# Expert keys of an attention-and-experts kernel by products of 512 columns, pooled values on 64x64 tiles, and another order of the first stage

## The chip, the cores and the metric

The kernel runs on one core of one Trainium2 chip. The metric is the time of one execution on the device in microseconds (us), lower is better. A core has five engines that work side by side, each in its own order: TensorE (PE in the profile, its weight loads PEld), VectorE (DVE), ScalarE (ACT), GpSimd (POOL) and SyncE (SP), which here issues all transfers between main memory and the on-chip memory (SBUF). TensorE writes its products to PSUM, which is divided into banks of 512 fp32 columns.

## What is computed

Eight batches of 576 positions go through an attention with 8 heads of 64 channels, and then through a gated mixture layer (512 channels, 1024 hidden). The reference, cut to what matters:

```python
q_d = q.reshape(B, H, Sd, factor, D).mean(axis=3)      # factor 4, Sd = 144; the same for k_d, v_d
out_d = sm_attn(q_d, k_d, v_d)                         # softmax attention on the pooled 144
out_up = np.repeat(out_d, factor, axis=2)
mask = np.abs(pos[:, None] - pos[None, :]) < factor    # local attention, |i - j| < 4
out_local = np.matmul(attn, v)
x = out_up + out_local                                 # heads side by side: (B, S, 512)
xk = mu_k * x + (1.0 - mu_k) * x_prev                  # x_prev: x shifted by one position
xr = mu_r * x + (1.0 - mu_r) * x_prev
k = np.maximum(xk @ w_k, 0.0)
v = k * k @ w_v
r = 1.0 / (1.0 + np.exp(-(xr @ w_r)))
return r * v
```

## The kernel before

**The work.** The 32 pairs of heads (4 for each batch) pass one after the other through an attention part, and the 18 chunks of 256 positions through an expert part. A pair n has its loads (`load_raw` for q and k, `load_v4` for the values to be pooled, `load_windows` for the local values), pooling on GpSimd, scores on TensorE (`score_pe`, `down_pe`, `down_last`), two softmaxes on the three other engines, `down_turn` (transposes on TensorE) and `av_pe`, the products with the values. From pair 5 on, `run_pe` puts the scores of pair n and the value products of pair n-1 into one run. `av_out` adds the upsampled pooled part and the local part to the tile xt of the batch.

**The expert part.** It works in fp32r, with each fp32 operand split into a high and a low part, and three products instead of one. For chunk c `mix_*` makes xk and xr (high and low), `k_pe(c, f)` makes the keys of one of 8 groups f of hidden channels: 12 products of 256 columns into one PSUM tile, (weight high, xk high), (weight high, xk low), (weight low, xk high) for each of 4 slices of the channels. `k_relu`, `k_high` (a square and a copy, ScalarE) and `k_low` (a difference, VectorE or GpSimd) make the squared keys in two parts, kh and kl. `v_pe(c, f)` adds 6 products of 512 columns to the two accumulators of the chunk, `r_pe` makes the gate with 24 products, `gate`, `store_mul` and `store_out` end the chunk. "k of f", "v of f" below stand for `k_pe(c, f)` and `v_pe(c, f)`.

**The weights.** 20 pieces (8 of w_k, 8 of w_v, 4 of w_r, 512 KB each) come as 64-bit numbers. For each, ScalarE (`weight_scale`) and VectorE (`weight_shift`, `weight_tail`, `weight_sign`, lines 287 to 296) make fp32 of it, and then the two parts.

**What sets the order.** All of these are tasks with an engine, a cost, a rank and the tiles they read and write. The class `Plan` lays them out in time by its own costs: at each step the task that can start first, and among those of one engine that can start by then the one with the lowest rank. Ranks are due times written out in the code (`PER`, `XLEAD`, `FETCH` and so on). The order found is then fixed on every engine by dependencies, so on the chip an engine takes its instructions in just that order, and one that waits holds up all behind it. The plan also gives each PSUM tile one of six banks; the scores have two more. `fill` puts products without use (`keep_warm`, tile ps_x) into TensorE's planned gaps of the first 100 us.

**The stages.** At first the loads, the weights and the four pairs of batch 0 run (nothing of the expert part can start before the xt of batch 0 is whole). Then the chunks run with the pairs of the following batches between them, and the last three or four chunks run alone.

## Time and profile before

| | us |
|---|---|
| median of 3 runs | 705.48 (703.69 to 705.82) |
| the profiled execution | 705.88 |
| its span, from the first to the last instruction | 703.9 |
| TensorE busy | 674.1 (96% of the span) |
| VectorE, ScalarE, GpSimd busy | 465.5, 439.3, 303.3 |
| transfers | 62.21 MB, mean 88 GB/s |

The table is that of one profiled execution beside the three timed ones. Busy times of TensorE hold its products without use too, and a busy TensorE is one in which some product is in the pipeline. 2.0 us of the profiled time lie outside the span.

### The profile page before, as it was taken

To read this page: it belongs to the slowest core of one execution; us is meant where nothing else is said; L and a number is where in the kernel's file an instruction comes from. 1 tells how busy PE (TensorE), PEld (TensorE's weight loads), DVE (VectorE), ACT (ScalarE), POOL (GpSimd) and SP (SyncE) were. 2 spreads that over 40 slices of the span, in tenths; PEclk is the share of its full clock that TensorE was granted. 3 is DMA by queue.
4 is the path that set the end of the run, shared out by engine and by line. 5 is a ranking of instruction groups with operands and counts; after the bars stand their busy time and mean duration, and the time that the engine had idled before them with its cause. 6 is when DMAs were issued, how large, how long until landed. Compare 5 with 4: busy or idle time off the path is not lost.

```text
span 703.9 us, 18635 instructions
## 1 busy us (share of the span) xinstructions
PE 674.1 (96%) x7467; PEld 576.9 (82%) x7467; DVE 465.5 (66%) x855; ACT 439.3 (62%) x1095; POOL 303.3 (43%) x374
## 2 busy tenths in 40 slices
PE   7888977999999999999999999999999999999997
PEld 5565866888888888888888888888888888988986
...
GB/s 149 181 197 273 221 148 132 124 79 116 68 114 75 107 56 128 54 93 44 87 87 52 59 115 88 88 77 104 71 101 40 53 2 31 1 30 31 1 32 31
DMA packets 221849, 62.21 MB, mean 88 GB/s; under 512 B 205122, under 2 KB 214594, under 8 KB 221762
## 3 DMA queue, kind: packets, MB, share of 16 engines
...
q14 instruction: 28, 0.23, 0.1%
...
## 4 chain that ended last, share of the span: by engine, by line
PE 69%; DVE 11%; ACT 5%; SPq 4%; POOL 4%; DMA 3%; issue 3%; DVEq 0%; POOLq 0%; ACTq 0%
PE ps_g L674 24%; PE acc L719 22%; PE ps_r L704 12%; PE ps_v L581 3%; SPq L335 3%; PE ps_a L449 2%; PE ps_v L575 2%; DMA v<-in_v_dram 1%; ACT ad L533 1%; ACT L533 1%; DVE ps_w L291 1%; PE ps_a L516 1%; DMA wv<-in_moe_w_v_dram 1%; DVE kl L693 1%; PE ps_a L509 1%
## 5 line engine op out<-in xcount | busy, mean ns | idle before, releaser
L674 PE MATMUL ps_g<-xkh,wk 128*128 128x256 f32 x1152 | 229.5, 285 | 2.9 <-ACT kk L679 2.0
L674 PEld LDWEIGHTS ps_g<-xkh,wk 128*128 128x128 f32 x1152 | 186.6, 190 | 11.4 <-ACT kk L679 4.9
L719 PE MATMUL acc<-wv,kh 128*128 128x512 f32 x576 | 181.2, 396 | 0.0
L674 PE MATMUL ps_g<-xkl,wk 128*128 128x256 f32 x576 | 162.6, 282 | 0.7 <-DVE xkl L666 0.7
L693 DVE TENSOR_TENSOR kl<-kk,kh 128x256 fp32r<-128x256 f32 x119 | 64.0, 538 | 118.0 <-ACT kh L686 110.8
L719 PEld LDWEIGHTS acc<-wv,kh 128*128 128x128 f32 x576 | 101.0, 189 | 18.9 <-issue 2.5
L674 PEld LDWEIGHTS ps_g<-xkl,wk 128*128 128x128 f32 x576 | 109.9, 191 | 3.9 <-DVE xkl L666 0.9
L719 PE MATMUL acc<-wv,kl 128*128 128x512 f32 x288 | 112.6, 391 | 0.1
L679 ACT ACTIVATE kk<-ps_g 128x256 f32<-128x256 f32 x144 | 54.5, 379 | 84.2 <-PE ps_g L674 77.9
L704 PE MATMUL ps_r<-wr,xrh 128*128 128x512 f32 x288 | 90.2, 394 | 1.7 <-POOL wr L323 1.4
L693 POOL TENSOR_TENSOR kl<-kk,kh 128x256 fp32r<-128x256 f32 x25 | 18.5, 742 | 124.2 <-PE acc L719 96.1
L719 PEld LDWEIGHTS acc<-wv,kl 128*128 128x128 f32 x288 | 54.1, 188 | 12.8 <-DVE kl L693 0.8
L686 ACT ACTIVATE kh<-kk 128x256 fp32r<-128x256 f32 x144 | 60.2, 418 | 4.6
L685 ACT ACTIVATE kk<-kk 128x256 f32<-128x256 f32 x144 | 60.1, 418 | 4.5
L704 PEld LDWEIGHTS ps_r<-wr,xrh 128*128 128x128 f32 x288 | 52.5, 188 | 12.4 <-POOL wr L323 1.8
L477 POOL TENSOR_TENSOR sm<-sm,mx 128x384 f32<-128x384 f32 x28 | 24.4, 873 | 83.1 <-DVE sd L539 60.6
L704 PE MATMUL ps_r<-wr,xrl 128*128 128x512 f32 x144 | 56.1, 390 | 0.0
L523 DVE TENSOR_REDUCE mxd<-ps_a 128x3 f32<-128x432 f32 x32 | 19.3, 604 | 48.8 <-PE ps_a L449 39.6
L422 POOL TENSOR_TENSOR v<-v 72x512 f32<-72x512 f32 x32 | 44.6, 1395 | 16.0 <-DMA v<-in_v_dram 15.8
L423 POOL TENSOR_TENSOR vd<-v 72x256 f32<-72x256 f32 x32 | 27.7, 866 | 51.0 <-PE ps_v L575 49.6
L413 POOL TENSOR_TENSOR tk<-kz 64x288 f32<-64x288 f32 (+1 forms) x56 | 41.9, 748 | 16.1 <-DVE kz L386 12.5
L533 ACT ACTIVATE ad<-ps_a,mxd 128x144 f32<-128x144 f32 x96 | 35.3, 376 | 20.3 <-DVE mxd L524 17.5
...
## 6 DMA issues: line engine op xcount, KB each, us to landing
...
qraw<-in_q_dram SPq DMA_DIRECT2D x128, 72.0 KB
kraw<-in_k_dram SPq DMA_DIRECT2D x128, 72.0 KB
...
```

The lines of the kernel that those rows point to most:

```text
L413: nc.gpsimd.tensor_tensor(out=tk[h], in0=k4[:, :, 0:2], in1=k4[:, :, 2:4], op=ALU.add)
L422: eng.tensor_tensor(out=v4[:, :, 0:128], in0=v4[:, :, 0:128], in1=v4[:, :, 128:256], op=ALU.add)
L423: eng.tensor_tensor(out=vd, in0=v4[:, :, 0:64], in1=v4[:, :, 64:128], op=ALU.add)
L477: nc.gpsimd.tensor_tensor(out=s3, in0=s3, in1=mx[:, :, None].broadcast_to([P, 12, 32]), op=ALU.subtract)
L533: nc.scalar.activation(ad[:, t, :], ps[:, t, :], AF.Exp, scale=1.0 / 128, bias=mx[:, t:t + 1], accum_out=sd[:, t:t + 1])
L674: nc.tensor.matmul(ps, w_k_part(p, f, w), y[:, p, :], start=(m == 0), stop=(m == len(mm) - 1))
L679: nc.scalar.activation(kk, kq[c, f], AF.Relu)
L685: nc.scalar.activation(kk, kk, AF.Square)
L686: nc.scalar.activation(kh, kk, AF.Copy)
L693: eng.tensor_tensor(out=kl, in0=kk, in1=kh.bitcast(F32), op=ALU.subtract)
L704: nc.tensor.matmul(ps, y[:, p, P * t:P * t + P], ws[f"r{p}"][:, w, :], start=(m == 0), stop=(m == len(mm) - 1))
L719: nc.tensor.matmul(accs[c][t], x[:, P * t:P * t + P], ws[f"v{f}"][:, w, :], start=(f == 0 and m == 0), stop=(f == NF - 1 and m == 2))
```

## The change

**Keys.** From chunk 2 on (`WIDE = 2`) the high and low parts of xk stand in one tile, and `k_pe` makes for each slice one product of 512 columns, weight high with both halves, into a PSUM tile of 2 x 256 columns, and then four of 256 columns, weight low with xk high, onto the first half. That is 8 products and 8 weight loads for each k in place of 12 and 12, of the same columns in sum. Since the two halves have to be added, ScalarE copies the second half to SBUF (`k_part`), VectorE adds the first one to it (`k_sum`, line 744), and `k_relu` then works on SBUF. The rest of the chain is as it was.

**Pooled values.** The 144 pooled positions were two blocks of 72. They now stand in a tile of 112 rows and one whose rows 96 to 127 hold the other 32, with rows 64 to 95 kept at zero, so that the products of `av_pe` have contractions of 64, 48 and 64 rows, and all lie on 64x64 tiles of TensorE, as the local products behind them do: 6 products in place of 4. The upper and the lower halves go to different PSUM tiles, and a new VectorE step (`av_two`, 144 columns) adds them. `load_v4` has two transfers in place of one, and `clear_v` sets the two value tiles to zero at the start.

**Order.** The table SHIFT changes ranks of tasks of the first chunks, pairs and weights; a few costs in the plan change too, and with the other tasks the whole order is laid out anew.

```diff
+WIDE = 2
 DXPOOL = 2
+KA = 112
+SHIFT = {
+    "av_up.5": -7.5, "c.0": 19.8, "c.1": 84, "c.3": 112.3, "down_sum.5": 35.8, "down_top.2": 2.2,
+    "down_top.4": 8.3, "fetch_weight.10": 4.7, "fetch_weight.12": 26.2, "fetch_weight.17": -87.2,
...
+    def shift(self, name, args):
+        if not args:
+            return SHIFT.get(name, 0.0)
+        i, more = args[0], args[1:]
+        full = f"{name}.{more[0]}" if name in ("mix_part", "mix_add", "mix_high", "mix_low") else name
+        kind = "c" if name in OF_CHUNKS else "w" if "weight" in name else "p"
+        if kind != "w" and i > (3 if kind == "c" else 9):
+            return 0.0
+        keys = [f"{kind}.{i}", f"{full}.{i}"]
+        if name in ("k_pe", "v_pe", "k_relu", "k_high", "k_low", "r_pe"):
+            keys.append(f"{name}.{i}.{more[0]}")
+        if name == "load_raw":
+            keys.append(f"{name}{more[0]}.{i}")
+        return sum(SHIFT.get(x, 0.0) for x in keys)
+
     def add(self, eng, us, rank, f, *args, r=(), w=(), new=(), dma=0.0, lock=None):
-        t = dict(eng=eng, us=us, rank=rank, f=f, args=args, new=list(new), dma=dma, deps=set(),
+        t = dict(eng=eng, us=us, rank=rank + self.shift(f.__name__, args), f=f, args=args, new=list(new), dma=dma, deps=set(),
                  id=len(self.tasks), name=f.__name__, lock=lock)
...
+    def clear_v():
+        for x in v4s:
+            nc.gpsimd.memset(x, 0.0)
...
         b, p = divmod(n, NP)
-        v4 = wp.tile([72, 4, 256], F32, tag="v4", name="v4", bufs=2)
+        v4 = v4s[n % 2]
         base = (b * H + 2 * p) * S * D
-        nc.sync.dma_start(v4, bass.AP(v.tensor, base, [[4 * D, 72], [288 * D, 4], [1, 4 * D]]))
+        nc.sync.dma_start(v4[0:KA, 0:2, :], bass.AP(v.tensor, base, [[4 * D, KA], [S * D, 2], [1, 4 * D]]))
+        nc.sync.dma_start(v4[96:P, 2:4, :], bass.AP(v.tensor, base + KA * 4 * D, [[4 * D, 32], [S * D, 2], [1, 4 * D]]))
         st.setdefault(n, {})["v4"] = v4
 
...
         d = st[n]
         if n < NP:
-            d["ps_t"] = [pp.tile([72, 288], F32, tag=plan.bank[f"pst{n}{kt}"], name="ps_t", bufs=1) for kt in range(2)]
+            d["ps_t"] = [pp.tile([P, 288], F32, tag=plan.bank[f"pst{n}{kt}"], name="ps_t", bufs=1) for kt in range(2)]
         else:
             ps = pp.tile([P, 1024], F32, tag="att", name="ps_t", bufs=1)
-            d["ps_t"] = [ps[0:72, 512 * kt:512 * kt + 288] for kt in range(2)]
-        for kt, ps in enumerate(d["ps_t"]):
-            ak = [d["ad"][:, t, 72 * kt:72 * kt + 72] for t in range(3)]
+            d["ps_t"] = [ps[:, 512 * kt:512 * kt + 288] for kt in range(2)]
+        for kt, (ps, ks) in enumerate(zip(d["ps_t"], (slice(0, KA), slice(16, 144)))):
+            d["ps_t"][kt] = ps = ps[0:ks.stop - ks.start]
+            ak = [d["ad"][:, t, ks] for t in range(3)]
...
-            nc.scalar.activation(d["adT"][:, kt, :], d["ps_t"][kt], AF.Copy)
+        d["adT"] = aT = wp.tile([P, 2, 288], F32, tag="adT", name="adT", bufs=1)
+        nc.scalar.activation(aT[0:KA, 0, :], d["ps_t"][0], AF.Copy)
+        nc.scalar.activation(aT[64:P, 1, :], d["ps_t"][1][64:P], AF.Copy)
...
 
         d = st[n]
         pv = [pp.tile([P, 432], F32, tag=plan.bank[f"pv{n}{x}"], name="ps_v", bufs=1) for x in ("", "b")]
-        for kt in range(2):
+        aT, up = d["adT"], slice(288, 432)
+        for r, h in enumerate((slice(0, 64), slice(64, KA))):
             for e in range(2):
-                nc.tensor.matmul(pv[0][64 * e:64 * e + 64, 288:432], d["vd"][:, 2 * e + kt, :],
-                                 d["adT"][:, kt, 144 * e:144 * e + 144], start=(kt == 0), stop=(kt == 1))
+                nc.tensor.matmul(pv[r][64 * e:64 * e + 64, up], d["vd"][h, e, :],
+                                 aT[h, 0, 144 * e:144 * e + 144], start=True, stop=(r == 0))
+        h = slice(64, P)
+        for e in range(2):
+            nc.tensor.matmul(pv[1][64 * e:64 * e + 64, up], d["vd"][h, 2 + e, :], aT[h, 1, 144 * e:144 * e + 144],
+                             start=False, stop=True)
         for g in range(NG):
             for r in range(2):
                 h = slice(64 * r, 64 * r + 64)
...
+    def av_two(n):
+        d = st[n]
+        nc.vector.tensor_tensor(out=d["up"], in0=d["pv"][1][:, 288:432], in1=d["up"], op=ALU.add)
 
...
-        h = wp.tile([P, NP, CT], F32R, tag=nm + "h", name=nm + "h", bufs=2 if nm == "xk" else 1)
-        nc.scalar.activation(h, mixes[c][nm], AF.Copy)
-        xs[c, nm] = [h]
+        x = wp.tile([P, 2, NP, CT], F32R, tag=nm, name=nm, bufs=2 if nm == "xk" else 1)
+        nc.scalar.activation(x[:, 0], mixes[c][nm], AF.Copy)
+        xs[c, nm] = x
...
-        xs[c, nm].append(lo)
+        x = xs[c, nm]
+        nc.vector.tensor_tensor(out=x[:, 1], in0=mixes[c][nm], in1=x[:, 0].bitcast(F32), op=ALU.subtract)
 
     def k_pe(c, f):
-        xh, xl = xs[c, "xk"]
-        ps = pp.tile([P, CT], F32, tag=plan.bank[f"g{c}.{f}"], name="ps_g", bufs=1)
-        mm = [(w, y, p) for p in range(NP) for w, y in ((0, xh), (0, xl), (1, xh))]
-        for m, (w, y, p) in enumerate(mm):
-            nc.tensor.matmul(ps, w_k_part(p, f, w), y[:, p, :], start=(m == 0), stop=(m == len(mm) - 1))
+        x = xs[c, "xk"]
+        if c < WIDE:
+            ps = pp.tile([P, CT], F32, tag=plan.bank[f"g{c}.{f}"], name="ps_g", bufs=1)
+            mm = [(w, y, p) for p in range(NP) for w, y in ((0, 0), (0, 1), (1, 0))]
+            for m, (w, y, p) in enumerate(mm):
+                nc.tensor.matmul(ps, w_k_part(p, f, w), x[:, y, p, :], start=(m == 0), stop=(m == len(mm) - 1))
+        else:
+            ps = pp.tile([P, 2, CT], F32, tag=plan.bank[f"g{c}.{f}"], name="ps_g", bufs=1)
+            for p in range(NP):
+                nc.tensor.matmul(ps, w_k_part(p, f, 0), x[:, :, p, :], start=(p == 0), stop=False)
+            for p in range(NP):
+                nc.tensor.matmul(ps[:, 0], w_k_part(p, f, 1), x[:, 0, p, :], start=False, stop=(p == NP - 1))
         kq[c, f] = ps
 
+    def k_part(c, f):
+        ps = kq[c, f]
+        kk = wp.tile([P, CT], F32, tag="kk", name="kk")
+        nc.scalar.activation(kk, ps[:, 1], AF.Copy)
+        kq[c, f] = ps, kk
+
+    def k_sum(c, f):
+        ps, kk = kq[c, f]
+        nc.vector.tensor_tensor(out=kk, in0=ps[:, 0], in1=kk, op=ALU.add)
+        kq[c, f] = kk
+
     def k_relu(c, f):
-        kk = wp.tile([P, CT], F32, tag="kk", name="kk")
-        nc.scalar.activation(kk, kq[c, f], AF.Relu)
-        kq[c, f] = kk
+        if c < WIDE:
+            kk = wp.tile([P, CT], F32, tag="kk", name="kk")
+            nc.scalar.activation(kk, kq[c, f], AF.Relu)
+            kq[c, f] = kk
+        else:
+            nc.scalar.activation(kq[c, f], kq[c, f], AF.Relu)
 
...
                 add("POOL", 0.1, R1, new_x, b, new=[(f"xt{b}", "xt")], w=[(f"xt{b}", i) for i in range(NP)])
+            add("DVE", 0.27, R1 + 2, av_two, n, r=[f"pv{n}b"], w=[f"up{n}"])
             add("DVE", 0.82, R1 + 2, av_out, n, r=[f"pv{n}", f"pv{n}b", f"up{n}"], w=[(f"xt{b}", p)])
...
                     held.pop(0)()
-            add("PE", 1.43, W, k_pe, c, f, r=[f"xkh{c}", f"xkl{c}"] + both(f"k{4 * (f // 4) + p}" for p in range(NP)),
+            add("PE", 1.43 if c < WIDE else 1.38, W, k_pe, c, f, r=[f"xk{c}"] + both(f"k{4 * (f // 4) + p}" for p in range(NP)),
                 new=[(f"g{c}.{f}", "bank")])
-            add("ACT", 0.38, W - 6, k_relu, c, f, r=[f"g{c}.{f}"], new=[(f"kk{c}.{f}", "kk")])
+            if c < WIDE:
+                add("ACT", 0.38, W - 6, k_relu, c, f, r=[f"g{c}.{f}"], new=[(f"kk{c}.{f}", "kk")])
+            else:
+                add("ACT", 0.38, W - 6, k_part, c, f, r=[f"g{c}.{f}"], new=[(f"kk{c}.{f}", "kk")])
+                add("DVE", 0.42, W - 6, k_sum, c, f, r=[f"g{c}.{f}"], w=[f"kk{c}.{f}"])
+                add("ACT", 0.38, W - 6, k_relu, c, f, w=[f"kk{c}.{f}"])
             add("ACT", 0.82, W - 6, k_high, c, f, w=[f"kk{c}.{f}"], new=[(f"kh{c}.{f}", "kh")])
             add(low_on(c, f), 0.42 if low_on(c, f) == "DVE" else 0.74, W - 6, k_low, c, f, r=[f"kk{c}.{f}", f"kh{c}.{f}"], new=[(f"kl{c}.{f}", "kl")])
...
                 else:
-                    add("PE", 3.3 if n < SPLIT else 2.85, at_run[n], run_pe, n, **join(av_of(n - 1), s))
+                    add("PE", 3.17 if n < SPLIT else 2.75, at_run[n], run_pe, n, **join(av_of(n - 1), s))
```

TensorE, beside one of the first chunks of the wide kind, before: a run (scores of one pair around the value products L575 and L581 of the pair before it), then v and the beginning of a k (L674).

```order
L509 MATMUL ps_a<-kd,qd_69 128x144
L575 MATMUL ps_v<-adT,vd 64x144 x4
L581 MATMUL ps_v<-bd,vw 64x48 x24
L516 MATMUL ps_a<-kd,qd_69 64x144 x4
L449 MATMUL ps_a<-kz_73,qT_76 32x64 x24
L719 MATMUL acc_2120<-wv_969,kh 128x512 x2
L719 MATMUL acc_2120<-wv_969,kl 128x512
L719 MATMUL acc_2121<-wv_969,kh 128x512 x2
L719 MATMUL acc_2121<-wv_969,kl 128x512
L674 MATMUL ps_g<-xkh,wk_988 128x256
L674 MATMUL ps_g<-xkl,wk_988 128x256
L674 MATMUL ps_g<-xkh,wk_988 128x256
```

After, at a run of the same stretch (L620 and L624 are the pooled values, L630 the local ones).

```order
L552 MATMUL ps_a<-kd,qd_69 128x144
L620 MATMUL ps_v<-adT,vd 64x144 x4
L624 MATMUL ps_v<-adT,vd 64x144 x2
L630 MATMUL ps_v<-bd,vw 64x48 x24
L559 MATMUL ps_a<-kd,qd_69 64x144 x4
L492 MATMUL ps_a<-kz_73,qT_76 32x64 x24
```

And a whole k after: first the four products of 512 columns, then the four of 256.

```order
L731 MATMUL ps_g<-xk,wk_1050 128x512
L731 MATMUL ps_g<-xk,wk_993 128x512
L731 MATMUL ps_g<-xk,wk_1047 128x512
L731 MATMUL ps_g<-xk,wk_1259 128x512
L733 MATMUL ps_g<-xk,wk_1050 128x256
L733 MATMUL ps_g<-xk,wk_993 128x256
L733 MATMUL ps_g<-xk,wk_1047 128x256
L733 MATMUL ps_g<-xk,wk_1259 128x256
```

What moved: the 12 narrow products of a k become 8, and between L552 and the scores only L620 and L624 stand where L575 stood.

VectorE, beside the same chunks, before: sums and transposes of a pair, and the kl of single k.

```order
L471 TENSOR_TENSOR sm<-ps_a,mask_75 128x384
L472 TENSOR_REDUCE mx<-sm 128x12
L539 TENSOR_SCALAR sd<-sd 128x3
L540 RECIPROCAL sd<-sd 128x3
L693 TENSOR_TENSOR kl<-kk,kh 128x256
L372 STREAM_TRANSPOSE qT_77<-qraw 128x576
L486 TENSOR_REDUCE ssum<-sm 128x12
L487 TENSOR_SCALAR ssum<-ssum 128x12
L488 RECIPROCAL ssum<-ssum 128x12
L386 STREAM_TRANSPOSE kz_74<-kraw 64x576 x2
L497 STREAM_TRANSPOSE at<-sm 128x384
L693 TENSOR_TENSOR kl<-kk,kh 128x256
```

After, in the same part: L744 is `k_sum`, L766 is `k_low`.

```order
L744 TENSOR_TENSOR kk<-ps_g,kk 128x256
L796 TENSOR_TENSOR sig<-acc_3149,sig 128x512
L719 TENSOR_TENSOR xr<-dx,xr 128x1024
L582 TENSOR_SCALAR sd<-sd 128x3
L583 RECIPROCAL sd<-sd 128x3
L685 TENSOR_TENSOR dx<-xt 128x1024
L766 TENSOR_TENSOR kl<-kk,kh 128x256
L744 TENSOR_TENSOR kk<-ps_g,kk 128x256
L529 TENSOR_REDUCE ssum<-sm 128x12
L530 TENSOR_SCALAR ssum<-ssum 128x12
L531 RECIPROCAL ssum<-ssum 128x12
L744 TENSOR_TENSOR kk<-ps_g,kk 128x256
```

What moved: each k has two VectorE steps now, and other work stands between them; ScalarE's relu, square and copy of that k wait for the first.

SyncE's transfers, from the values of pair 2 on, before (wk, wv, wr are weights, vw the local values, v the values to be pooled).

```order
L344 DMA v_321<-in_v_dram 72x4x256
L335 DMA qraw<-in_q_dram 32x18x32 x4
L335 DMA kraw<-in_k_dram 32x18x32 x4
L278 DMA wv_446<-in_moe_w_v_dram 128x1024
L358 DMA vw<-in_v_dram 32x12x64 x4
L278 DMA wv_475<-in_moe_w_v_dram 128x1024
L278 DMA wv_479<-in_moe_w_v_dram 128x1024
L278 DMA wv_483<-in_moe_w_v_dram 128x1024
L344 DMA v_489<-in_v_dram 72x4x256
L358 DMA vw<-in_v_dram 32x12x64 x4
```

After, from behind the q of pair 3 on.

```order
L320 DMA wv_395<-in_moe_w_v_dram 128x1024
L377 DMA kraw<-in_k_dram 32x18x32 x4
L386 DMA v_78<-in_v_dram 112x2x256
L387 DMA v_78<-in_v_dram 32x2x256
L320 DMA wv_466<-in_moe_w_v_dram 128x1024
L401 DMA vw<-in_v_dram 32x12x64 x4
L386 DMA v_79<-in_v_dram 112x2x256
L387 DMA v_79<-in_v_dram 32x2x256
L401 DMA vw<-in_v_dram 32x12x64 x4
L320 DMA wk_520<-in_moe_w_k_dram 128x1024
L320 DMA wv_524<-in_moe_w_v_dram 128x1024
L401 DMA vw<-in_v_dram 32x12x64 x4
```

What moved: ahead of the last vw of batch 0 there are ten weights now (six of them above this piece) and eight before, but the v of pair 3 has no row of three weights just ahead of it any more.

## Rows read from the trace of the kernel before

**Rows 1.** Windows: length; PE, PEld, DVE, ACT, POOL busy us; clock; DMA share; GB/s.

```profile
0.00:74.00 74.00, 60.75 (x836) 42.69 (x836) 51.24 (x98) 40.38 (x101) 36.14 (x56) 0.98 0.93 198
74.00:120.00 46.00, 36.88 (x593) 31.16 (x595) 38.06 (x57) 30.57 (x81) 41.07 (x44) 0.96 0.96 166
120.00:150.00 30.00, 29.07 (x383) 25.22 (x377) 17.75 (x37) 22.98 (x55) 19.69 (x27) 0.95 0.58 114
150.00:600.00 450.00, 447.24 (x5095) 388.77 (x5087) 321.81 (x599) 297.47 (x753) 203.47 (x245) 1.00 0.37 76
600.00:704.00 104.00, 100.19 (x600) 89.04 (x598) 36.63 (x66) 47.88 (x108) 2.95 (x4) 1.00 0.06 21
```

**Rows 2.** The page's chain that ended last, shares by line.

```profile
PE ps_g L674 24%; PE acc L719 22%; PE ps_r L704 12%; PE ps_v L581 3%; SPq L335 3%; PE ps_a L449 2%; PE ps_v L575 2%; DMA v<-in_v_dram 1%; ACT ad L533 1%; ACT L533 1%; DVE ps_w L291 1%; PE ps_a L516 1%; DMA wv<-in_moe_w_v_dram 1%; DVE kl L693 1%; PE ps_a L509 1%
```

**Rows 3.** The chain in order of time: start, us, what.

```profile
210.42 2.89 PE ps_g L674 x24
213.31 2.79 PE acc L719 x12
...
652.78 2.80 PE ps_g L674 x24
655.58 2.75 PE acc L719 x12
```

**Rows 4.** Timeline of TensorE in one run: start, us, instructions.

```profile
310.05 0.71 PE L575 MATMUL ps_v<-adT,vd 72*64 72x144 f32 x8
310.69 0.92 PE L581 MATMUL ps_v<-bd,vw 64*64 64x48 f32 x48
311.43 0.44 PE L516 MATMUL ps_a<-kd,qd 64*64 64x144 f32 x8
311.80 0.88 PE L449 MATMUL ps_a<-kz,qT 128*32 128x64 f32 x48
```

**Rows 5.** Timeline of TensorE ahead of the first k.

```profile
63.52 10.53 PE L314 MATMUL ps_x<-nidn 128*128 128x512 f32 x43
73.97 0.35 PE L674 MATMUL ps_g<-xkh,wk 128*128 128x256 f32 x1
```

**Rows 6.** Groups by line and form: busy us, mean ns, idle before.

```profile
L693 DVE TENSOR_TENSOR kl<-kk,kh 128x256 fp32r<-128x256 f32 x119 | 64.0, 538 | 118.0 <-ACT kh L686 110.8 <-PE acc L719 4.9 <-POOL kd L414 0.9
...
L685 ACT ACTIVATE kk<-kk 128x256 f32<-128x256 f32 x144 | 60.1, 418 | 4.5
...
L679 ACT ACTIVATE kk<-ps_g 128x256 f32<-128x256 f32 x144 | 54.5, 379 | 84.2 <-PE ps_g L674 77.9 <-DVE xk L647 2.9 <-DVE kl L693 1.7
...
L611 DVE TENSOR_TENSOR xt<-ps_v,up 128x288 f32<-128x288 f32 x64 | 25.9, 446 | 1.2 <-ACT up L603 1.2
```

**Rows 7.** Windows: two stretches of 36 us at batch boundaries.

```profile
220.00:256.00 36.00, 35.13 (x409) 30.27 (x408) 32.90 (x56) 27.53 (x68) 20.85 (x22) 1.00 0.40 84
292.00:328.00 36.00, 35.22 (x316) 30.84 (x316) 31.70 (x56) 26.98 (x67) 17.20 (x21) 1.00 0.36 79
```

**Rows 8.** The chain in order of time, ahead of the first k.

```profile
46.00 9.75 DMA v<-in_v_dram
...
69.90 1.79 DVE xk L657
```

**Rows 9.** Whom TensorE waited for from 74 to 150 us: us, times, longest.

```profile
PE ps_t L556 <- POOL ad L544: 3.0, 3, 1.3
PE ps_a L454 <- issue: 2.3, 1, 2.3
PE ps_v L581 <- ACT bd L503: 1.8, 1, 1.8
```

**Rows 10.** Timeline behind the last k.

```profile
695.80 0.28 PE L674 MATMUL ps_g<-xkh,wk 128*128 128x256 f32 x1
...
697.49 0.42 DVE L693 TENSOR_TENSOR kl<-kk,kh 128x256 fp32r<-128x256 f32 x1 [2.45 <-ACT kh L686]
...
698.67 0.62 PE L719 MATMUL acc<-wv,kh 128*128 128x512 f32 x2
```

38 lines of the change are left out of this document (20 added, 18 removed), and 13 rows, old and new, of the table SHIFT.

## The prediction

> **What bounds the kernel now.** The windows by stage come first, since the mean over the span hides that the stages have different limits [rows 1]. From 150 us to 600 us TensorE is busy 447.24 of 450 us at the full clock, and from 600 us on all but the last 4 us; VectorE has 321.81 of 450 us there, 72%, ScalarE 66%. From 74 to 120 us it is another picture: TensorE 36.88 of 46 us, the transfer engines 0.96, VectorE 38.06 of 46. Before 74 us there is no expert product at all. The chain that ended last says the same from the other side: k 24%, v 22% and r 12% of the span lie on it, all TensorE's [rows 2]. So there are two places where time can be won. One is the length of TensorE's own work from about 120 us on: each us taken off a k or a run is a us off the end, as long as nobody lets TensorE wait. The other is TensorE's empty time before that: 74 to 150 us it lacks 9.1 + 0.9 = 10.0 us [rows 1], mostly in short waits for the softmax of the next pair (GpSimd, ScalarE) and one of 2.3 us for which the profile shows no releaser [rows 9].
>
> **Keys.** Two stretches show both widths side by side. At 210 us a product of 256 columns takes 2.89 / 24 = 0.1204 us and one of 512 takes 2.79 / 12 = 0.2325 us; in the last stage they take 2.80 / 24 = 0.1167 and 2.75 / 12 = 0.2292 us [rows 3]. A k was 12 narrow products; it is now 4 wide and 4 narrow ones. Beside the attention this is 1.445 us before and 4 x 0.2325 + 4 x 0.1204 = 1.412 us after, 33 ns less; in the last stage 1.400 and 1.384 us, 16 ns less. Of the 128 changed k some 104 stand beside attention and 24 in the last stage: 104 x 0.033 + 24 x 0.016 = 3.8 us. The columns streamed stay the same, so what is won is only the fixed part of a product, and that is why it is so little for a third of the instructions. The bound on one side is 33 ns on all of them, 4.2 us. On the other side stands an unknown: the wide product reads its columns as two runs of 256 that lie apart. The nearest row for a broken run is the product without use, which reads four runs of 128: 43 of them take 73.97 - 63.52 = 10.45 us, 0.243 us each, 10 ns above the 0.2325 of a plain one [rows 5]. If two runs cost as much, a k is 4 x 10 - 33 = 7 ns longer, 0.9 us lost in all. I take the 3.8, since those 43 products differ in more than the runs (each opens and closes its own sum).
>
> On the fixed part the Trainium skill (TensorE: Matmul & The Clock Gate, section "Back-to-back issue gap") gives a smaller price: a gap of N / 2.4 plus about 2.5 ns for isolated products at the full clock. By it a pair of narrow products put together saves 2.5 ns, 128 x 4 x 2.5 ns = 1.3 us by an estimate from that page, in place of 3.8. The rows here stand against it, 0.1167 us where that formula gives 0.109.
>
> **What the halves cost elsewhere.** Each k gets a ScalarE step and a VectorE step. The copy is priced as the old relu from PSUM, 379 ns, which it replaces there; the relu now reads SBUF like the square, 418 ns, and is the addition [rows 6]: 128 x 0.42 = 54 us more of ScalarE. `k_sum` reads one operand in PSUM and one in SBUF as `av_out` does, 446 ns for 288 columns, so 0.40 us for 256; the bound above is `k_low`, two operands in SBUF, 538 ns [rows 6]. That is 51 us of VectorE, at most 69. `av_two`, 144 columns, is half of an `av_out` piece, 0.22 us, 7 us in all. From 150 to 600 us about 100 of the k and 25 of the pairs lie: VectorE goes to (322 + 40 + 6) / 444 = 83%, ScalarE to (297 + 42) / 444 = 76%. Both are still hidden behind TensorE on the mean. If that cover were gone, what is late is kl: v of that f waits for it, and behind this v stands all of TensorE's queue.
>
> The chain behind a k gets longer by the two steps, 0.42 + 0.40 and two handovers, about 1 us. In the middle three pieces or more of 1.4 us stand between k of f and v of f in the order, and one us fits. At the end it is closest: the last narrow product starts at 695.80, kl starts at 697.49 and ends at about 697.9, and the last v needs its kh at 698.67 [rows 10]. One us later is 698.9 for kl, whose product comes 0.45 us behind 698.67. I allow 0.2 us.
>
> On `k_sum` a rule of the Trainium skill (SBUF — State Buffer, section "SBUF: two separate sides") bears: an operation of VectorE with two inputs in SBUF and one of GpSimd lock each other out for a whole instruction. `k_sum` has only one such input, so by this rule it is not drawn out as `k_low` is; by the other price VectorE would have 18 us more.
>
> **Pooled values.** In a run the four products L575 take 310.69 - 310.05 = 0.64 us, the 24 local ones 0.74, and the four of the same 144 columns on 64x64 tiles (L516) 311.80 - 311.43 = 0.37 [rows 4]. Both L575 and L516 are followed by products on tiles of another shape, L581 is not. L575 has four passes one behind the other on each half of the columns (two products of two passes), L516 two; so 4p + s = 0.64 and 2p + s = 0.37 give p = 0.135 us a pass and s = 0.10 us for the change of shape. After the change the lower rows still have four passes, but no change of shape behind them: 0.10 us less a pair. Below, nothing is won if the new first product pays it in another place; above, if the upper rows run on by two passes with nobody in their way, 0.10 + 2 x 0.135 = 0.37 us, which the order does not allow, since the local products alternate between the halves. From 120 us on there are 26 of these: 2.6 us, 0 to 4. The transposes (L556 to L558) stream as many columns as before, the copies too. The second transfer of v4 is one more issue for SyncE, which waits most of the time by then; the two memsets are GpSimd's before its first input.
>
> **Order of the first stage.** The pieces shown of SyncE say what moves. Before, the v of pair 3 was issued at 46.00 us behind three weights in a row and took 9.75 us to land, and the first sum of xk on VectorE is at 69.90 us with VectorE full all the way between [rows 8]. After, that v stands behind one weight, and two weights more are taken before the last vw. Weights taken early are VectorE work done in its idle first 40 us (51.24 of 74 us busy up to 74 [rows 1]). Against this, two weights of 512 KB at 198 GB/s [rows 1] put the last input of batch 0 back by 2 x 2.6 = 5.3 us, if transfers are the limit, and at 0.93 they nearly are. After the first k the best that can be won are the 10.0 us of idle. I take a quarter of it, 2.5 us won; bounds 10 won and 5.3 lost.
>
> **New waits.** At batch boundaries VectorE has 32.90 and 31.70 of 36 us [rows 7]; 8 `k_sum` and 2 `av_two` add 3.6, which makes 36.5 and 35.3. There TensorE already lacks 0.87 and 0.78 us. With six such boundaries and 0.4 us more at each I put 2.4 us; 0 to 12.
>
> **Sum.** -3.8 - 2.6 - 2.5 + 2.4 + 0.2 = -6.3 us. The profiled execution took 705.88 us, 1.98 outside its span, 0.40 above the median: 699.6 for it, 699.2 as a median.
>
> **The rivals.**
> - *VectorE becomes the bound at the boundaries.* For it: over 36 us of work in a window of 36, in fixed order, with kl queued behind sums of 1 us and more. Against it: the windows between have room, and xk is made ahead. If each of six boundaries loses 2 us: 705.5 - 6.4 - 2.5 + 12 + 0.2 = 708.8. It decides, to slower, above (2.1 + 8.9) / 6 = 1.8 us for each.
> - *The first stage gets later.* The two weights ahead of the last vw cost their 5.3 us and win nothing: 705.5 - 6.4 + 2.6 + 5.3 = 707.0, no change that can be told or a little slower. VectorE's lead with the weights speaks against it.
> - *The first stage wins its waits.* All 10.0 us go and no new waits come: 705.5 - 6.4 - 10 = 689.1. For it: these waits are short and each is a matter of order. Against: transfers at 0.96 share.
> - *The wide product is no quicker.* Two runs cost what two products did: 705.5 - 2.6 - 2.5 + 2.4 + 0.2 = 703.0. For it: the fixed part is all that is won, and the broken run of [rows 5] has one of its own. Against: that run has four pieces, this one two. By the gap of the page named above the time would lie between this and the forecast, at 701.7.
>
> **How the numbers follow.** A difference under 0.3%, 2.1 us, cannot be told from none here. Chances: the forecast 0.42, VectorE the bound 0.12, a later first stage 0.14, a first stage without waits 0.18, no quicker product 0.14. The time is that of the forecast, 699. The range leaves out half of the fastest case and most of the slowest: 689.5 to 707.5; the forecast alone has 695 to 703. Faster gets the forecast, the fast case and half of the last, 0.67; within 0.3% comes from the last two kinds, 0.16; slower from VectorE and part of the later first stage, 0.17.
>
> **What the profile after would show.** Wide products of ps_g near 0.23 us apart and narrow ones near 0.118; from the first pooled product to the first local one 0.54 us; VectorE near 83% from 150 to 600 us and TensorE short of that stretch by about 5 us; the first k near 74 us, and less idle TensorE from there to 150 us. I am wrong if waits of ps_g or acc for kl or kk add up to more than 8 us, if wide products lie 0.24 us apart, or if the first k moves by more than 4 us either way.

## The result and the profile after

The changed kernel takes 697.26 us (median of 4, 695.45 to 698.06) beside 704.94 for the one before on the same chip: ratio 0.9875, 95% interval 0.9852 to 0.9898. The profiled execution is the fastest of them, 695.45 us with a span of 693.7, so the two traces lie 10.2 us apart and the medians 7.7.

Windows of the changed kernel, columns as in [rows 1]:

```profile
0.00:74.00 74.00, 62.02 (x867) 46.17 (x868) 56.43 (x106) 43.48 (x106) 41.32 (x62) 0.98 0.97 204
74.00:120.00 46.00, 42.53 (x652) 36.45 (x651) 39.41 (x70) 36.13 (x91) 43.15 (x49) 1.00 0.94 170
120.00:150.00 30.00, 29.68 (x441) 25.79 (x441) 24.23 (x48) 21.96 (x62) 20.63 (x26) 1.00 0.61 127
150.00:600.00 450.00, 445.95 (x4703) 375.25 (x4695) 359.53 (x712) 335.80 (x848) 198.29 (x239) 1.00 0.33 74
```

From 74 to 120 us TensorE now lacks 3.5 us in place of 9.1. VectorE has 359.53 of 450 us (80%), ScalarE 75%, and TensorE lacks 4.05 us there, 1.3 more than before. What it still waits for from 74 to 150 us (us, times, longest), beside [rows 9]:

```profile
PE ps_a L497 <- issue: 1.5, 1, 1.5
PE ps_a L552 <- POOL kd L457: 1.5, 2, 1.1
PE ps_g L727 <- DVE sig L796: 0.5, 1, 0.5
PE acc L792 <- DVE kl L766: 0.3, 1, 0.3
```

TensorE's timeline ahead of the first k, beside [rows 5]:

```profile
65.82 5.16 PE L356 MATMUL ps_x<-nidn 128*128 128x512 f32 x22
70.82 0.28 PE L727 MATMUL ps_g<-xk,wk 128*128 128x256 f32 x1
```

The first k comes 3.2 us earlier, in one execution of each kernel. In the runs below that have the same transfers (6, 7, 9, 11 and 12) it comes between 70.6 and 74.0, so 3.2 us are no more than the scatter. What TensorE has done by a given time tells more. Its products of v (tile acc) in the first 150 us, before and then after:

```profile
0.00:150.00 150.00, 16.40 (x66) 0.97 0.87 172
0.00:150.00 150.00, 21.30 (x84) 0.99 0.89 178
```

The changed kernel is 18 of these ahead, and by the same count 2 k (16 in place of 14), the scores and the transposes of one pair and a part of its values. At 0.23 us a product, 1.4 us a k and 2 to 3 us for the pair this is 9 to 10 us, by an estimate from the rows. The two traces end 10.2 us apart: nearly all of it is won ahead of 150 us, and behind that the two kernels take about as long. The chain in the last stage (start, us, what), beside the lower pair of [rows 3]:

```profile
642.85 0.92 PE ps_g L731 x4
643.77 0.47 PE ps_g L733 x4
...
645.63 2.75 PE acc L792 x12
```

Wide products lie 0.230 us apart, narrow ones 0.117. The k of the kernel before at 210 us ([rows 3], upper pair) begins thus:

```profile
210.25 0.36 PE L674 MATMUL ps_g<-xkh,wk 128*128 128x256 f32 x1
210.46 0.29 PE L674 MATMUL ps_g<-xkl,wk 128*128 128x256 f32 x1
```

Its first product, behind a block of transposes, takes 0.21 us up to the next, and the 23 others up to v at 213.14 take 0.117 each. TensorE in one run, beside [rows 4]:

```profile
298.71 0.48 PE L620 MATMUL ps_v<-adT,vd 64*64 64x144 f32 x8
299.00 0.21 PE L630 MATMUL ps_v<-bd,vw 64*64 64x48 f32 x2
...
300.31 0.41 PE L492 MATMUL ps_a<-kz,qT 128*32 128x64 f32 x13
```

From the first pooled product (L620) to the first local one (L630) it is 0.29 us (0.64 before). From the first pooled product to the first local score (L492) it is 1.60 (1.75 before): most of what the head of the run wins is given back among the local products, between which those of the lower rows (L624) now stand. The transposes of a pair go the other way. The kernel before and then the changed one, first transpose and what follows the last:

```profile
325.17 0.27 PE L556 MATMUL ps_t<-idn,ad 128*72 128x128 f32 x1
...
325.80 0.47 PE L719 MATMUL acc<-wv,kh 128*128 128x512 f32 x1
```

```profile
310.94 0.27 PE L600 MATMUL ps_t<-idn,ad 128*112 128x128 f32 x1
...
311.68 0.48 PE L731 MATMUL ps_g<-xk,wk 128*128 128x512 f32 x1
```

0.63 us has become 0.74 with the same columns streamed. Groups of the changed kernel, beside [rows 6]:

```profile
L766 DVE TENSOR_TENSOR kl<-kk,kh 128x256 fp32r<-128x256 f32 x119 | 65.5, 551 | 40.0 <-ACT kh L759 38.6 <-PE ps_v L630 0.3
L744 DVE TENSOR_TENSOR kk<-ps_g,kk 128x256 f32<-128x256 f32 x128 | 52.6, 416 | 56.5 <-ACT kk L739 55.9
```

`k_sum` takes 416 ns (0.40 had been put), and VectorE's free time ahead of `kl` is down from 118.0 to 40.0 us. The mean of `kl` hides two levels: from 150 to 600 us, where GpSimd is busy 44% of the time, and then from 600 us on, where it has 2.32 of 94 us:

```profile
L766 DVE TENSOR_TENSOR kl<-kk,kh 128x256 fp32r<-128x256 f32 x89 | 52.4, 589 | 18.2 <-ACT kh L759 17.4
L766 DVE TENSOR_TENSOR kl<-kk,kh 128x256 fp32r<-128x256 f32 x24 | 10.2, 426 | 18.7 <-ACT kh L759 18.5
```

`k_sum` takes 414 and 424 ns in the two. The two stretches of [rows 7]:

```profile
220.00:256.00 36.00, 36.00 (x428) 30.20 (x428) 33.87 (x62) 29.94 (x72) 20.44 (x23) 1.00 0.40 87
292.00:328.00 36.00, 36.00 (x389) 30.39 (x388) 31.83 (x64) 27.14 (x69) 11.35 (x14) 1.00 0.30 71
```

TensorE lacks nothing in either. But the batch boundaries lie elsewhere now: the sums of xk for the chunk in which a batch begins, at 227.14 and 299.95 us before, come at 216.35 and 281.65. The stretches of 36 us around them in which VectorE is fullest:

```profile
210.00:246.00 36.00, 36.00 (x389) 29.91 (x388) 34.81 (x63) 28.93 (x67) 19.40 (x24) 1.00 0.41 89
274.00:310.00 36.00, 36.00 (x286) 30.34 (x285) 34.33 (x64) 29.06 (x74) 14.20 (x19) 1.00 0.37 80
```

VectorE has 34.81 and 34.33 us there (36.5 and 35.3 had been put), and TensorE lacks nothing.

### The profile page after: what moved, and what is told of

It reads as the page before. It is cut to its first block, busy times and chain, and to the rows that moved or that the text cites. A ratio compares the mean times of both kernels' runs of the same rounds, so it can differ in the third digit from the quotient of the medians.

```text
span 693.7 us, 18197 instructions
## 1 busy us (share of the span) xinstructions
PE 670.1 (97%) x7084; PEld 558.9 (81%) x7084; DVE 521.2 (75%) x1015; ACT 488.3 (70%) x1223; POOL 305.7 (44%) x376
## 4 chain that ended last, share of the span: by engine, by line
PE 77%; DVE 6%; POOL 5%; DMA 3%; ACT 3%; issue 2%; SPq 2%; DVEq 0%; POOLq 0%; ACTq 0%
PE acc L792 25%; PE ps_g L731 16%; PE ps_r L777 14%; PE ps_g L733 8%; PE ps_v L630 3%; PE ps_a L492 3%; PE ps_v L620 2%; DMA wk<-in_moe_w_k_dram 1%; PE ps_a L559 1%; PE ps_t L600 1%; PE ps_t L602 1%; POOL ad L587 1%; PE ps_a L552 1%; DMA vw<-in_v_dram 1%; SPq L377 1%
## 5 line engine op out<-in xcount | busy, mean ns | idle before, releaser
L731 PE MATMUL ps_g<-xk,wk 128*128 128x512 f32 x512 | 142.0, 399 | 1.9 <-DVE xk L719 1.8
L731 PEld LDWEIGHTS ps_g<-xk,wk 128*128 128x128 f32 x512 | 92.6, 189 | 20.9 <-issue 2.4
L777 PE MATMUL ps_r<-wr,xr 128*128 128x512 f32 x432 | 104.3, 395 | 0.0
L766 DVE TENSOR_TENSOR kl<-kk,kh 128x256 fp32r<-128x256 f32 x119 | 65.5, 551 | 40.0 <-ACT kh L759 38.6
L744 DVE TENSOR_TENSOR kk<-ps_g,kk 128x256 f32<-128x256 f32 x128 | 52.6, 416 | 56.5 <-ACT kk L739 55.9
L777 PEld LDWEIGHTS ps_r<-wr,xr 128*128 128x128 f32 x432 | 79.8, 188 | 17.3
L733 PEld LDWEIGHTS ps_g<-xk,wk 128*128 128x128 f32 x512 | 79.0, 189 | 11.2
L733 PE MATMUL ps_g<-xk,wk 128*128 128x256 f32 x512 | 81.6, 282 | 0.0
L766 POOL TENSOR_TENSOR kl<-kk,kh 128x256 fp32r<-128x256 f32 x25 | 21.6, 864 | 120.1 <-ACT kh L759 120.0
L753 ACT ACTIVATE kk<-kk 128x256 f32<-128x256 f32 x128 | 52.8, 412 | 28.7 <-DVE kk L744 27.9
L758 ACT ACTIVATE kk<-kk 128x256 f32<-128x256 f32 x144 | 60.1, 418 | 4.3
L466 POOL TENSOR_TENSOR vd<-v 128x256 f32<-128x256 f32 x32 | 31.5, 985 | 49.5 <-PE ps_v L624 48.1
L520 POOL TENSOR_TENSOR sm<-sm,mx 128x384 f32<-128x384 f32 x28 | 24.0, 857 | 55.6 <-DVE mx L515 35.3
L440 POOL TENSOR_TENSOR tq<-qT 128x288 f32<-128x288 f32 x32 | 21.7, 678 | 57.0 <-DVE qT L415 54.3
L465 POOL TENSOR_TENSOR v<-v 128x512 f32<-128x512 f32 x32 | 45.5, 1421 | 2.6 <-DMA v<-in_v_dram 1.4
```

The costliest lines, as they stand in the source:

```text
L465: eng.tensor_tensor(out=v4[:, :, 0:128], in0=v4[:, :, 0:128], in1=v4[:, :, 128:256], op=ALU.add)
L731: nc.tensor.matmul(ps, w_k_part(p, f, 0), x[:, :, p, :], start=(p == 0), stop=False)
L733: nc.tensor.matmul(ps[:, 0], w_k_part(p, f, 1), x[:, 0, p, :], start=False, stop=(p == NP - 1))
L744: nc.vector.tensor_tensor(out=kk, in0=ps[:, 0], in1=kk, op=ALU.add)
L753: nc.scalar.activation(kq[c, f], kq[c, f], AF.Relu)
L758: nc.scalar.activation(kk, kk, AF.Square)
```

## The experiments

Theory: the prediction's terms, each with its own size. Main rival: the terms don't add up, because a changed kernel under the old rules gets another order, and the table's worth is that it mends it. Times are medians; the ratio is to the kernel before on the same chip. The medians come from several chips, and by the ratios a difference between two runs comes out up to 0.8 us otherwise.

**1. Without the table.**

```
-SHIFT = { "av_up.5": -7.5, ... }
+SHIFT = {}
```

> The changed kernel with its table of rank shifts emptied; wide keys and pooled tiles stay. Theory 1 (from the two traces: k started 3.2 us earlier, and TensorE's empty time and half-clock time between 74 and 150 us shrank by about as much again): the table is worth 5 to 8 us, so the kernel takes 702 to 705 us against 697.3 for the changed kernel and 704.9 for the one before; first k at or behind 74 us; TensorE's stretch from 150 to 600 us is unchanged in kind. Theory 2 (the prediction's term): the table is worth 2.5 us, 699.8. Theory 3 (keys and pooled values carry all of it): no change, 697.3.

Measured: 715.93 us, ratio 1.0134 (1.0111 to 1.0157): 18.7 us slower than with the table, and slower than the kernel before. Both theories with a small price for the table fall, and mine was too small as well. Windows of this kernel, and under them of the changed one:

```profile
120.00:160.00 40.00, 37.05 (x603) 31.22 (x601) 21.44 (x43) 23.54 (x57) 21.26 (x30) 1.00 0.46 104
160.00:166.20 6.20, 0.17 (x6) 0.11 (x2) 5.93 (x13) 4.15 (x14) 1.86 (x3) 0.76 0.46 114
166.20:180.00 13.80, 11.89 (x148) 9.78 (x149) 10.89 (x19) 7.75 (x21) 7.73 (x9) 0.61 0.48 94
180.00:200.00 20.00, 20.00 (x206) 16.88 (x205) 16.30 (x35) 14.24 (x33) 8.99 (x11) 1.00 0.32 61
```

```profile
120.00:160.00 40.00, 39.68 (x583) 34.34 (x582) 34.00 (x64) 30.23 (x81) 28.35 (x36) 1.00 0.62 128
160.00:180.00 20.00, 20.00 (x206) 16.89 (x205) 19.12 (x38) 16.34 (x41) 9.14 (x13) 1.00 0.44 98
```

TensorE's timeline without the table, at the hole:

```profile
159.79 0.27 PE L476 MATMUL ps_a<-kz,qT 128*32 128x64 f32 x5
166.09 0.46 PE L584 MATMUL ps_t<-idn,ad 128*112 128x128 f32 x1 [6.03 <-POOL ad L571]
...
168.68 0.85 PE L536 MATMUL ps_a<-kd,qd 128*128 128x144 f32 x2 [0.92 <-ACT adT L593]
...
171.68 1.60 PE L614 MATMUL ps_v<-bd,vw 64*64 64x48 f32 x47 [0.99 <-ACT bd L530]
...
175.19 1.97 PE L715 MATMUL ps_g<-xk,wk 128*128 128x512 f32 x4
...
177.46 1.09 PE L715 MATMUL ps_g<-xk,wk 128*128 128x512 f32 x4
```

Between two runs of attention no expert product is left: those of chunk 1 are used up, and xk of chunk 2 is still being made, on VectorE among others (5.93 of 6.20 us busy). TensorE waits 6.03 us for the softmax of a pair and then for its other steps, and behind the empty stretch the granted clock is 0.61 for 13.8 us, with four wide products in 1.97 us where the next four take 1.09: part of it was at the lower of the two levels (1.2 of 2.4 GHz). With the table the products of chunk 1 are used up about as early (the last one starts at 154.70 us, here at 157.01), but xk of chunk 2 is ready: its last step on VectorE starts at 150.00 us, here at 170.56. From 154.92 us on six k of chunk 2 stand between the pairs, and 20.00 of 20 us are busy at full clock.

This trace is that of the slowest execution of run 1 and lies 23.5 us behind that of the changed kernel. Some 12 to 13 us of them are the hole: 6.0 us empty, 1.9 of further waits, and 11.89 us of work at 0.61 of the clock, which loses 4.6 by an estimate. Another 8 us, by an estimate from the products done by 150 us (75 of v and 15 k here, 84 and 16 with the table, and one to two pairs' steps), lie ahead of it.

**2 and 3. One part alone under the old rules.** The kernel before with the wide keys alone, and with the pooled tiles alone. Both have the joined tile for the high and low parts of xk.

```
 # keys alone: k_pe with ps[:, 2, CT], k_part, k_sum; the rest as before
 # pooled alone: load_v4, pool_v, down_turn, down_copy, av_pe, av_two, and the joined tile of xk; the rest as before
```

> The kernel before with the wide keys alone (joined xk tile, k_part, k_sum), the order as the old rules make it, without the table. Wide keys and new tiles together without the table took 715.9. Theory 1 (the prediction's sum: keys -3.8, waits +2.4): 703.5. Theory 2 (the new VectorE and ScalarE steps disturb the order that the rules make, and the table repairs it): 710 or more, with empty TensorE between 150 and 300 us as in the run without the table.

> The kernel before with the pooled values on 64x64 tiles alone, the order as the old rules make it, without the table. Theory 1 (1.0 us as the runs in an unchanged order and the traces have it): 703.9 to 704.5, no difference that can be told. Theory 2 (prediction's term): 702.5. Theory 3 (this is the part that disturbs the order that the rules make: av_two on VectorE, another bank held for longer): 708 or more.

Measured: 713.64 us, 1.0117 (1.0091 to 1.0144), and 720.45 us, 1.0207 (1.0180 to 1.0234). Each part alone makes the kernel slower than it was, by 8.1 and 14.9 us, where I had given them gains. The hole is at the same place. TensorE's timeline with the keys alone, then with the pooled tiles alone:

```profile
165.39 0.43 PE L577 MATMUL ps_t<-idn,ad 128*72 128x128 f32 x1 [4.29 <-POOL ad L565]
```

```profile
161.54 0.46 PE L584 MATMUL ps_t<-idn,ad 128*112 128x128 f32 x1 [6.03 <-POOL ad L571]
```

So it is no price of the wide products or of the tiles, which differ in the two: the rules put the pairs and the chunks in an order with that hole. What the two share with run 1 is the joined tile, and with it one dependency of the plan. The steps of xr of chunks 0 and 1 (`mix_part`) waited for the high part of xk; now they wait for the joined tile, and so for the low part, which is written last:

```
-  ([f"xkh{c}"] if nm == "xr" and c < ACTMIX else [])
+  ([f"xk{c}"] if nm == "xr" and c < ACTMIX else [])
```

The plan can be laid out from a kernel's code without the chip. For the kernel before with nothing changed but this dependency, from the high part to the low one, it leaves TensorE empty for 4.9 us ahead of the transposes of the same pair. That is what the plan of run 2 has there too, where the chip shows 4.29; the plans of runs 1 and 3 have 6.3, where the chip shows 6.03. With this one dependency put back on the high part, the plans of all three have no empty stretch there. No run timed such an order: that a good part of the table's worth is the mending of this one dependency is likely, and not shown.

**4 and 5. The old form of one part, planned anew with the table.**

```
-WIDE = 2
+WIDE = 18
 # and, in the other kernel, the old pooled values with their old entries in the plan
```

> The changed kernel with narrow key products in every chunk, so without k_part and k_sum too. Theory 1 (start-to-start times of the trace: keys 4.7 us shorter, new waits 1.3 us): 697.3 + 3.4 = 700.7 us, VectorE and ScalarE in 150 to 600 us back at 72% and 66%. Theory 2 (the waits at VectorE eat what the products win): 697.3 or less. Theory 3 (the gap of 2.5 ns for a product, as the Trainium skill's page TensorE: Matmul & The Clock Gate has it, section Back-to-back issue gap): 1.3 us from the keys, so 697.3 as well.

> The changed kernel with the pooled values as they were before (72 rows, one bank, no av_two); keys and order stay. Theory 1 (the two traces: from the first pooled product to the first score 1.747 us before and 1.598 after, but the transposes with the start of what follows 0.629 before and 0.741 after): only 0.15 - 0.11 = 0.04 us a pair, 26 pairs, so 1.0 us: 698.3. Theory 2 (the prediction's term, 0.10 us a pair and nothing for the transposes): 2.6 us, 699.9. Theory 3 (0.30 us a pair, the distance from the first pooled to the first local product): 7.8 us, 705.1. The table of shifts was searched for the new tiles, so the stretch up to 150 us is read apart.

Measured: 709.78 us, 1.0046 (1.0029 to 1.0063), and 733.76 us, 1.0378 (1.0351 to 1.0405). Neither prices the part: the plan's tasks and costs change with it, and the table was made for another plan (the first k came at 73.2 and 83.8 us). The part has to be exchanged with every instruction left in its place, as in the next runs.

**6. Split products, order held.**

```
-  matmul(ps, w_k_part(p, f, 0), x[:, :, p, :], start=(p == 0), stop=False)
+  for y in range(2):
+      matmul(ps[:, y], w_k_part(p, f, 0), x[:, y, p, :], start=(p == 0 and y == 0), stop=False)
```

> The changed kernel with each wide key product split into two narrow ones that fill the two halves of the same bank; k_part, k_sum and every other instruction stay in their places on every engine. It prices the width alone. Theory 1 (prediction's term, 33 ns a k beside attention and 16 in the last stage): 3.8 us longer, 701 us. Theory 1b (start-to-start times of the two traces): 4.7 us, 702. Theory 2 (the gap of 2.5 ns a product, by the Trainium skill's page TensorE: Matmul & The Clock Gate, section Back-to-back issue gap): 1.3 us, 698.6. Theory 3 (VectorE and ScalarE are the bound behind 150 us, TensorE's work is cover): under 1 us.

**7. Old keys, order held.** `k_pe` sums 12 narrow products into `ps[:, 0]`, `k_part` is the relu from it, `k_sum` and the later relu are gone.

> The changed kernel with the old keys in its own order: 12 narrow products into one half of the bank, relu straight from it, no copy of a half and no sum; all other instructions stay in their places on every engine. Splitting the products alone cost 0.4 to 1.7 us, and 53 us more of VectorE cost 21. Theory 1 (the prediction's: the new steps are hidden behind TensorE, apart from some waits of 2.4 us): products 1.7 us longer, waits 1 to 2.4 us shorter, so 696 to 698, no difference that can be told; VectorE at 69 to 70% of 150 to 600 us. Theory 2 (rival: VectorE has no slack left in the changed kernel, so the 53 us that go come back at the rate at which those that were added cost): 697 + 1.7 - 10 to 20 us, below 690, the fastest kernel of all. Theory 3 (the wide keys pay as the prediction's term says): 699 to 701.

**8 and 9. Old pooled values, order held; with the old transfer and with the new ones.**

```
-  v4[0:KA, 0:2, :] and v4[96:P, 2:4, :]            # 224 KB and 64 KB
+  v4, bass.AP(..., [[4 * D, 72], [288 * D, 4], [1, 4 * D]])   # 288 KB, in run 8 only
+  down_turn, down_copy, av_pe, pool_v as before; av_two as a max that changes nothing
```

> The changed kernel with the old products, transposes and transfers of the pooled values put in the places of the new ones; the plan, its costs and the order on every engine stay (the VectorE step of the pair stays as one that leaves the values as they are). Theory 1 (traces: 0.15 us a run won, 0.11 us a pair lost in the transposes): 1.0 us longer, 698.3. Theory 2 (prediction's term): 2.6 us, 699.9. Theory 3 (0.30 us a pair): 7.8 us, 705.

> The changed kernel with the old products, transposes and sums of the pooled values, but with its own two transfers of v4 (112 and 32 rows): the products then read rows 0 to 71 of the four blocks, which don't hold the values that belong there, so part of the output is not the reference's; the work on each engine is that of the old form. With the old single transfer the same kernel took 702.6 us, 5.3 more than the changed kernel, of which 0.9 us lay behind the v of chunk 1 and the rest ahead of it. Theory 1 (the rest is the transfer: one of 288 KB over 72 rows holds up SyncE's queue in the first 30 us, where the weight of r was issued at 27.15 in place of 23.36 us): with the new transfers 697.5 to 699, first k at 71 to 74 us, wr issued near 23 to 24.5 us. Theory 2 (the old products and transposes themselves delay the first stage): 702 to 703, first k near 77 us.

**10. Transposes of 104 columns.**

```
-KA = 112    ... slice(0, KA), slice(16, 144)
+KA = 104    ... slice(0, KA), slice(40, 144)
```

> The changed kernel with the two pieces of the transposed weights 104 and 104 columns wide (rows 0 to 103, and 40 to 143) in place of 112 and 128, the pooled rows split at 104 to match; the order stays. If a transpose costs by the width of the block that TensorE loads as its weights (theory 1: 0.629 us at 72 to 0.741 at 112 and 128, so 0.06 us a pair less), 1 to 2 us shorter, 695.5 to 696.3, and a block of transposes with the start of what follows at about 0.69 us. If not (theory 2: it is the new tile of 64 rows that the transposes wait for), no change.

**11. One run of 512 columns.** `x = tile([P, NP, 2, CT])` in place of `[P, 2, NP, CT]`.

> The changed kernel with xk and xr laid out so that a wide product reads its 512 columns as one run and not as two of 256 that lie apart. Theory 1 (prediction: the two runs cost nothing): no change, 697.3, wide products 0.229 to 0.233 us apart as now. Theory 2 (a broken run costs some ns as in the product without use, 10 ns for four runs): up to 512 x 5 ns = 2.6 us shorter, wide products nearer to 0.225 us.

What runs 6 to 11 measured. The last column is one profiled execution each: from the first product of v of chunk 1 to the end of the last product, by TensorE's timeline, which leaves out the first stage. In the changed kernel and in run 6 the granted clock averages 0.95 from 530 to 565 us and 1.00 in the others; 5% of 35 us, 1.7 us by an estimate, is taken off there.

| | median us | ratio (95%) | first k | chunk 1's v to end |
|---|---|---|---|---|
| changed | 697.26 | 0.9875 (0.9852 to 0.9898) | 70.82 | 562.4, less 1.7: 560.7 |
| 6 split products | 697.68 | 0.9892 (0.9878 to 0.9906) | 74.03 | 564.0, less 1.7: 562.3 |
| 7 old keys | 694.78 | 0.9843 (0.9820 to 0.9867) | 71.10 | 560.6 |
| 8 old pooled, old transfer | 702.61 | 0.9950 (0.9932 to 0.9969) | 77.06 | 561.6 |
| 9 old pooled, new transfers | 697.85 | 0.9890 (0.9870 to 0.9909) | 70.63 | 561.6 |
| 10 transposes of 104 | 697.33 | 0.9875 (0.9858 to 0.9892) | 72.23 | 560.1 |
| 11 one run | 695.76 | 0.9861 (0.9849 to 0.9874) | 70.80 | 560.9 |

*Run 6*: the width is worth 1.6 us in the trace and 0.4 in the medians (1.2 by the ratios), which that measurement does not tell from nothing. My 3.8 falls. *Run 7*: the keys as a whole are worth nothing here; without them the kernel is 2.5 us faster by the medians, with intervals that overlap. What the wide products win, the two new steps take. Windows, 150 to 600 us:

```profile
150.00:600.00 450.00, 447.62 (x5127) 395.24 (x5127) 326.33 (x612) 297.39 (x751) 196.35 (x240) 1.00 0.34 74
```

VectorE is back at 326.33 us (73%, not the 69 to 70 I expected), and TensorE lacks 2.38 us in place of 4.05. That VectorE's work comes back at the rate of run 12 (theory 2 there) falls too.

*Runs 8 and 9*: products, transposes and sums of the new form are worth 0.6 us by the medians and 0.9 in the trace, the 1.0 that the two traces gave. The other 4.8 us (4.2 by the ratios) are the transfer alone. SyncE's queue in run 8, the issues of v4, of the next weights of k and of r:

```profile
13.15 0.79 SPq L386 DMA_DIRECT2D v<-in_v_dram  x2
...
21.08 3.29 SPq L320 DMA_DIRECT2D wk<-in_moe_w_k_dram  x2
...
27.15 0.50 SPq L320 DMA_DIRECT2D wr<-in_moe_w_r_dram  x1
```

And in run 9, with 112 and 32 rows in place of 72:

```profile
20.39 1.35 SPq L320 DMA_DIRECT2D wk<-in_moe_w_k_dram  x2
...
22.81 1.03 SPq L320 DMA_DIRECT2D wr<-in_moe_w_r_dram  x1
```

The weight of r is issued 4.3 us earlier and the first k comes 6.4 us earlier, with the same bytes to move; at 77.06 it lies 3 us behind the latest of the runs with the new transfers. These rows don't show why one transfer over 72 rows holds the queue longer. The Trainium skill (DMA: Bandwidth & Descriptors, section "Why a DMA increments its semaphore by 16 and not by 1") says that a transfer runs on the largest number of engines, up to 16, that divides its slowest dimension on both sides. By it 72 rows would have 12 engines, 112 and 32 rows 16; the delay agrees in its direction, and no run here shows the count.

*Run 10*: a block of transposes with the start of what follows takes 0.697 us (median of 23) beside 0.739 at 112 and 128 columns of weights and 0.629 at 72, so the width of the weights is the price; 0.04 us a pair, 1 us in all, is below what the medians tell. The transfers become 104 and 40 rows with this edit, so its median holds that change too. How the width comes in, the load of the weights shows: 191 ns on average for the short product at 128 columns, 143 at 72. The Trainium skill (TensorE: Matmul & The Clock Gate, section "LDWEIGHTS (loading the stationary operand)") has columns / 1.2 ns, by an estimate 47 ns more, and the traces agree with that difference for this load; the loads ahead of the two longer products differ by 77 and 24 ns. *Run 11*: wide products stay 0.23 us apart, so the two runs of 256 cost nothing; the 1.5 us between the medians has overlapping intervals.

**12. The sum made twice, order held.**

```
+  nc.vector.tensor_tensor(out=ps[:, 1], in0=ps[:, 0], in1=kk, op=ALU.add)
   nc.vector.tensor_tensor(out=kk, in0=ps[:, 0], in1=kk, op=ALU.add)
```

> The changed kernel with the VectorE sum of the halves made twice for each wide k (the first time into the half of the bank that has been read, where nobody reads it), the order left as it is: some 128 x 0.42 = 53 us more of VectorE, about 90% of 150 to 600 us. Theory 1 (the prediction's own: VectorE is hidden, with a few tenths of a us lost at a batch boundary): VectorE has slack left, the cost is below 6 us, 698 to 703. Theory 2 (rival, VectorE is already the bound at the boundaries): each of the 16 doubled k near the six or seven boundaries puts its 0.42 us straight on the end, and the rest of the chain kk to kl too: 710 or more.

Measured: 718.90 us, 1.0174 (1.0155 to 1.0192), 21.6 us more for 54.4 us of VectorE (128 times 425 ns). Theory 1 falls. The windows, 150 to 600 us, and three of TensorE's waits there:

```profile
150.00:600.00 450.00, 434.30 (x4567) 359.30 (x4566) 385.25 (x795) 324.65 (x820) 196.40 (x238) 1.00 0.33 74
```

```profile
PE ps_t L600 <- POOL ad L587: 3.9, 5, 2.0
PE ps_g L731 <- DVE kk L745: 3.9, 6, 1.0
PE ps_v L620 <- DVE kk L745: 1.8, 2, 0.9
```

With 86% of VectorE's time taken, TensorE lacks 15.7 us. The changed kernel stands at 80%, where run 7 shows little to be won by less work. But the second sum does more than fill VectorE: it stands in the chain from each k to its kl, it holds the PSUM bank 0.43 us longer, and two of the waits shown are for what stands behind it (`kk` L745). This run does not tell the load from the longer chain.

## Why the prediction was right, and where not

The time forecast, 699.0 with 695 to 703 for the likeliest case, held; several terms under it did not, and their errors cancelled. That is luck: the keys and the pooled values, put at 6.4 us together, are worth 1 us or less with the new steps counted, and the first stage, put at 2.5, won 9 to 10 in the traces and made up for them.

- **Keys, -3.8.** Mis-sized: 1.6 for the width. The step that failed is the price of 33 ns beside attention: 0.1204 us for a narrow product was a mean over 24 of them, of which the first, behind a block of transposes, took 0.21 and the others 0.117. The last stage's 16 ns on all 128 k gives 2.0, close to the 1.6. The gap of the Trainium skill (TensorE: Matmul & The Clock Gate, section "Back-to-back issue gap") gave an estimate of 1.3; that difference agrees with the runs, while the durations themselves do not (0.117 us a narrow product, 0.109 by the formula).
- **Steps of the halves.** The sum was priced rightly (0.40 us, measured 0.416), the later relu too. `kl`, with two operands in SBUF, takes 551 ns at the same size, 589 beside a busy GpSimd and 426 beside an idle one. The rule of the Trainium skill (SBUF — State Buffer, section "SBUF: two separate sides") that an operation of VectorE with two inputs in SBUF and one of GpSimd that reads SBUF lock each other out agrees with these rows. Hidden the steps were not: run 7 shows that they take what the width wins.
- **End, +0.2.** From 600 us on the trace has no wait of TensorE.
- **Pooled values, -2.6.** Sign right, size 0.6 to 0.9. The head of the run won more than said (0.29 us where I put 0.54), the whole run 0.15 us a pair; that the transposes cost nothing more was wrong, they take 0.11 us a pair back.
- **The transfers of v4.** Not in the sum ("one more issue for SyncE, which waits most of the time by then"). In the changed kernel's order their shape is worth 4.8 us. This is the term that was missing.
- **First stage, -2.5, and new waits, +2.4.** The step that failed is to price the table as a gain in the first stage beside the other terms. Without it the rest of the change takes 18.7 us more under the old rules; in the trace over half of the difference is one hole near 160 us with the low clock behind it, and a third lies ahead of 150 us. TensorE's empty time from 74 to 150 us went from 10.0 to 3.8 us, and 1.3 us more are lost behind 150: these two answer to -2.5 and +2.4 as the traces show them, both with the table's help. Products without use fill planned gaps and count as busy, so empty time does not tell all; by the work done, the first stage as a whole won 9 to 10 us, with the shape of the transfers in it.
- **Rivals.** VectorE as the bound may have been near: a little more of its work in the chain behind each k (run 12) costs 21.6 us. Without the table a time on that side comes out (715.9), though by the hole near 160 us and not at the boundaries that I named. That the wide product is no quicker is nearly true, and it cost little. (In the first rival the 8.9 should be 6.4 + 2.5 - 0.2 = 8.7; the limit of 1.8 us stays.)

The worths don't add up: table 18.7, transfers 4.8, pooled products 0.6, keys nothing or less, each undone by itself from the changed kernel, beside 7.7 won in all. Which of the table's entries do it was not tried. The fastest median is run 7, the table and the pooled tiles with the old keys; it beats the kernel before, and is not told apart from the changed one.
